# A transformer block on one core: the third part of each output block, the loads of key stacks and the key differences placed behind the maxima's parts, with SyncE's queue in the program's order during attention

## The chip, the cores and the metric

The kernel runs on one core of one Trainium2 chip. The metric is the device time of one execution in microseconds; the time before is the median of three runs. A profile is one execution recorded by the hardware profiler, and all rows below are from it. The engines are PE (TensorE), DVE (VectorE), ACT (ScalarE) and POOL (GpSimd); SP (SyncE) only issues DMAs here.

## The reference

One transformer block on 2048 rows of 576 numbers:

```
x  = A_x
h  = x + attention(layernorm(x), wqkv, wo)      # 32 heads of 18 columns, full softmax
h2 = h + (gelu(n @ w_gate) * (n @ w_up)) @ w_down    with n = layernorm(h), 4608 hidden columns
```

The result is float32. The kernel gets this accuracy with pairs of float16 numbers (high and low part), and with seven products in place of eight in the second half.

## The kernel before, in words

The program has three stages. Up to about 203 us it normalises the rows and makes queries, keys and values. Then comes attention, up to about 1405 us, and then the gated products to the end.

**Attention** is a loop over 32 blocks, n = 4g + qc: eight groups g of four heads, and in each group four blocks qc of 512 queries. A block has 16 steps kt, one for each 128 keys. In a step PE makes the scores of the four heads (`score`, L704, into PSUM banks), ACT takes their exponentials (L714, L716), and PE multiplies them with the values (`weigh`, L725) into two accumulators.

The exponentials need the largest score of each query ahead of time. `maxima` is a generator that runs one and a half blocks ahead of the scores: PE makes products (`max_bank`, L642), DVE takes their maxima (L656, L654), and ACT helps with L650. In step kt = 9 of block n the first piece taken from it calls `max_finish(n + 1)`: one more reduction on DVE (L667), three small operations that scale and split the result (L670 to L672, on POOL), a DMA that transposes it (L674, tile mT), and four small DMAs that put it into two extra rows of the query stacks (L680, A<-mT or W<-mT). The first score of block n + 1 reads these rows.

**Output of a block** is `out_block(n)`, a generator in three parts, run during block n + 1. Part one copies the accumulators (L739 on ACT, L741 on DVE), adds them on POOL (L742) and fetches the row of sums as tile rc with a DMA (L747). Part two inverts the sums (POOL, L754 to L758; in the last four blocks DVE, L760), writes them to DRAM (L762) and reads them back spread over partitions (L763, nat<-rc). Part three multiplies with them and splits the result (POOL, L767 to L769; in the last two blocks DVE, L771 to L773), and writes it to its place in X with four to nine DMAs (L782, L785, L786). Before, part two is taken behind step kt = 3 and part three behind kt = 5 (kt = 6 from block 29 on).

**Key stacks.** `load_stacks(g + 1)` issues 12 DMAs on SP and 12 on POOL (L593, L594), `load_ends` 8 on SP (L615), and `key_steps` five POOL operations (L622 to L625), 8 DMAs to DRAM (L628, kd<-nat) and 3 back (L630, nat<-kd). They fill the set of the next group; the first to read it are its maxima, from block 4g + 2, step 9 on.

**Behind the maxima.** From block 30, step 9 on, there are no maxima left, and each step takes one product of the output matrix: `wo_pairs` for 8 row tiles, then `wo_block(2)` for 4 more from step 15 of block 31 on. Both are `wo_tiles`: its local `fetch` (L849) loads a row tile of x into one of two buffers, `xbs` (one in A, one in WK). The tile's two products (L325) are added to it by DVE (L859), and then tile k + 2 is fetched. The products of `wo_pairs` use one PSUM bank in turn, those of `wo_block(2)` four. `rows` cuts finished rows into float16 parts on DVE (L917 to L921) and turns them with DMA transposes (L947).

**What sets the order.** PE, ACT, DVE and POOL run in the order in which the program is written. SP's queue does so up to L1312 and again from L1382 on, behind the loop. In between, a scheduler orders SP's DMAs by its own estimate: it may issue a DMA earlier than it is written. Each queue runs strictly in order: a DMA whose data is not ready holds up those behind it.

Of the kernel before, what the change touches and what calls it, by code (L numbers as in the profile page):

```python
# [28 lines left out]
MSC = 4096.0  # L29
# [3 lines left out]
def tile_block(  # L33
# [18 lines left out]
    nc = tc.nc  # L52
# [4 lines left out]
    NT = S // P  # L57
    TB = min(512, S)
    NB = S // TB
# [6 lines left out]
    NG = H // 4  # L66
# [16 lines left out]
    def of_pair(ins, banks, write):  # L83

        x = ins.ins
        mine = str(x.engine)
        for e in sorted(engines_of_pair - {mine}):
            keep = [o for b in banks for group in last_use[b][: 1 + write] for o in group if str(o.engine) == e]
            tc.declare_no_dep(x, group=f"pair_{e}", keep=keep, reason="the other bank of the pair")
        tc.add_to_no_dep_group(f"pair_{mine}", x)  # L90
        engines_of_pair.add(mine)
        return x
# [234 lines left out]
    def run(it):  # L327
        for _ in it:
            pass
# [8 lines left out]
    def take(it, n=1):  # L338
        for _ in range(n):
            next(it, None)  # L340
# [103 lines left out]
    in_order = ExitStack()  # L444
# [124 lines left out]
    def half(j, rows):  # L569
        return slice(64 * j, 64 * j + rows)  # L570
# [29 lines left out]
    LOWEST = -3.0e38  # L600
# [18 lines left out]
    def key_steps(g):  # L619

        for d, e in zip(dif, ends):
            nc.gpsimd.tensor_sub(d, e[:, 1::2], e[:, ::2])  # L622
        nc.gpsimd.tensor_add(dif[0], dif[0], dif[1])
        nc.gpsimd.tensor_copy(parts_d[0], dif[0])
        nc.gpsimd.tensor_sub(parts_d[1], dif[0], parts_d[0])  # L625
        for k, d in zip(kd, parts_d):
            for s in range(DQ):
                nc.sync.dma_start(k[:, :, s], d[s * DH : (s + 1) * DH])  # L628
        for i, k in enumerate((kd[0], kd[1], kd[0])):
            nc.sync.dma_start(steps[g % 2][i * DH : (i + 1) * DH],  # L630
                              k.rearrange("r h s i -> r h (s i)"))
# [32 lines left out]
    def max_finish(n, mx):  # L664
        g, qc = divmod(n, NB)
        m = small.tile([P, 4, TPB], F32, tag="m", name="m")
        nc.vector.tensor_reduce(m, mx.rearrange("p t h c -> p h t c"), axis=AX.X, op=ALU.max)  # L667
        mm = mms[n % 2]
        hst = mm[:, : 8 * TPB].rearrange("p (h s t) -> p h s t", h=4, s=2)
        nc.gpsimd.tensor_scalar_mul(m, m, 1 / MSC)  # L670
        nc.gpsimd.tensor_copy(hst[:, :, 0], m)
        nc.gpsimd.tensor_sub(hst[:, :, 1], m, hst[:, :, 0])  # L672
        mT = small.tile([P, 1, P], F16, tag="mT", name="mT")
        nc.sync.dma_start_transpose(mT, mm)  # L674
        for pr in range(2):
            Q = sets[g % 2][pr][0]
            for j in range(2):
                k = (4 * pr + 2 * j) * TPB
                row = 64 * j + R1
                nc.sync.dma_start(Q[row : row + 2, qc * TB : (qc + 1) * TB],  # L680
                                  mT[k : k + 2 * TPB, 0])

    NPE = 4
# [8 lines left out]
    def bank_at(i):  # L692

        return pair[:, i] if i < 2 else (singles[:3] + quads[1:2])[i - 2]

    def score(n, kt, heads, bank):

        g, qc = divmod(n, NB)
        mm = []
        for i, hh in enumerate(heads):  # L700
            pS = bank_at(bank + i)
            Q, K = sets[g % 2][hh // 2]
            r = half(hh % 2, R1 + 2)
            mm += [nc.tensor.matmul(pS[c : c + CT, :TB], K[r, kt * P + c : kt * P + c + CT],  # L704
                                    Q[r, qc * TB : (qc + 1) * TB], start=True, stop=True)
                   for c in range(0, P, CT)]
        of = tuple(range(bank, bank + len(heads)))
        if bank < 2:
            xs = [of_pair(m_, (of[k // 4],), True) for k, m_ in enumerate(mm)]
            for k, b in enumerate(of):  # L710
                wrote_pair((b,), xs[4 * k : 4 * k + 4])
        pe = pes[(2 * kt + heads[0] // 2) % NPE]
        if len(heads) == 2:
            act = nc.scalar.activation(pe, pair, AF.Exp, scale=ex_reg)  # L714
        else:
            act = nc.scalar.activation(pe[:, heads[0] % 2], bank_at(bank)[:, :TB], AF.Exp, scale=ex_reg)  # L716
        if bank < 2:
            read_pair(of, of_pair(act, of, False))

    def weigh(n, kt, accs, q):  # L720
        qs = slice(q * TB // 2, (q + 1) * TB // 2)
        for i, acc in enumerate(accs):
            ks = slice(64 * i, 64 * i + 64)
            for hh in range(4):
                nc.tensor.matmul(acc[CT * hh : CT * hh + CT, qs],  # L725
                                 Vg[n // NB][ks, kt * G4 + hh * VC : kt * G4 + hh * VC + CT],
                                 pes[(2 * kt + hh // 2) % NPE][ks, hh % 2, qs],
                                 start=(kt == 0 and q == 0), stop=(kt == NT - 1 and q == 1))
# [61 lines left out]
    NS = NG * NB  # L790
# [5 lines left out]
    def maxima():  # L796

        for n in range(NS):
            mx = small.tile([P, TPB, 4, NB], F32, tag="mx", name="mx")
            over, both = ("over", "both") if n else ("one", "one")  # L800
            if n:
                nc.gpsimd.memset(mx[:, :, 0, 1::2], LOWEST)
            for u in range(0, UPS, 2):
                t, k = divmod(u, NB)
                for unit in ((over, t, k + 1, 0), ("one", t, k, 1), ("one", t, k + 1, 1), ("one", t, k, 2),
                             ("one", t, k, 3), ("one", t, k + 1, 2), ("one", t, k + 1, 3), (both, t, k, 0)):
                    max_bank(n, mx, *unit, bank=bank_now[0])
                    yield
            max_finish(n, mx)
# [496 lines left out]
    qk_tiles(3, 4, 5)  # L1306
    load_stacks(0)
    load_ends(0)
    key_steps(0)
    load_w(of, wo, nc.gpsimd)  # L1310
    sums = chain(norm_wo(), raw_norms())
    sp_order.close()  # L1312
# [15 lines left out]
    halves = deque([None, None])  # L1328
    LAST_MAX = (NS - 1) * NT - 7
    rows = rows0()  # L1330
    for n in range(NS):
        g, qc = divmod(n, NB)
        late = n > NS - NB
        for kt in range(NT):
# [13 lines left out]
                else:  # L1348
                    take(side)
            halves += [(n, kt, accs, q) for q in range(2)]  # L1350
            if n and kt in ((2 if n == NS - 1 else 3, 6) if late else (3, 5)):
                take(ob)
            if n * NT + kt == LAST_MAX - 2:
                fill = wo_pairs(ring(singles[:1]))
# [10 lines left out]
            if g == 0 and qc == 0 and kt == NT - 1:  # L1365
                run(fill)
                init_set(sets[1])
            if g + 1 < NG and kt == 2 and qc == (1 if g == 0 and NB > 1 else 0):
                load_stacks(g + 1)
                load_ends(g + 1)  # L1370
            if g + 1 < NG and kt == 9 and qc == (1 if g == 0 and NB > 1 else 0):
                key_steps(g + 1)
            if n == 2 and kt == 4:
                side = prepare_wo()
            if n == NS - NB and kt == 2:
# [2 lines left out]
            if n == NS - NB and kt == 8:  # L1378
                side = chain(split_early(0, 0, lambda: load_matrix(w_up, 0, nc.gpsimd)), pause(2),
                             split_early(0, 1, lambda: load_matrix(w_gate, 1, nc.gpsimd)),  # L1380
                             pause(2), until_ready(second))
    in_order.enter_context(tc.manual_schedule(engines={EngineType.SP}))  # L1382
    run(side)
    for half_ in halves:
        weigh(*half_)
# [106 lines left out]
```

## Time and profile before

| | us |
|---|---|
| median of 3 runs | 2631.65 (2628.14 to 2634.61) |
| the profiled execution's own time | 2628.84 |
| its span, first to last instruction | 2627.1 |
| PE busy | 2548.7 (97%) |
| DVE busy | 2003.7 (76%) |
| ACT busy | 1651.6 (63%) |
| POOL busy | 858.0 (33%) |
| mean granted TensorE clock | 0.992 |

In the rows, "us" stamps run from the span's start. A row of the timeline gives start, length, engine, line, operation, tiles, and how often; in brackets the idle time of the engine before it and what ended it. SPq rows are DMA issues on SP's queue, not the transfers. A row of the windows gives the stretch and its length, then busy time and count for each engine, then the granted clock (PEclk), the DMA engines' share and GB/s.

### The profile page before, as it was taken

The page shows a single profiled execution, that of the slowest core. Times are in us where ns is not written, and L with a number is a line of the kernel's source. Part 1 is how long each engine was busy: PE and PEld are TensorE (multiplying, and loading weights), DVE is VectorE, ACT ScalarE, POOL GpSimd, SP SyncE. Part 2 cuts the span into 40 slices and gives each one's busy share as a digit, 9 for nine tenths or more (in the row PEclk, how much of TensorE's full clock was granted, in tenths as well). Part 3 has the DMA queues.
Part 4 walks back from the last instruction along what each step waited for, and adds up shares of the span by engine and source line. Part 5 has one row for each costly group of instructions (what it writes and reads, how often), then busy time and mean ns, then how long its engine had stood idle before and what let it go on. Part 6 is the DMA issues. An engine that isn't in the chain of part 4 may idle for free.

```text
span 2627.1 us, 96403 instructions
## 1 busy us (share of the span) xinstructions
PE 2548.7 (97%) x41245; PEld 1446.6 (55%) x41245; DVE 2003.7 (76%) x3888; ACT 1651.6 (63%) x2898; POOL 858.0 (33%) x1176
## 2 busy tenths in 40 slices
PE   8999899999999999999999999999999999999999
PEld 4645455555555555555555555555555555555555
DVE  8479899999999999999957765656565656565653
ACT  6229899999999999999965433333333333333332
POOL 4301532332323232433676432222222222222221
PEclk9999999999999999999999999999999999999999
DMA  8621010101101010101126410101010101011110
GB/s 225 153 78 46 18 47 21 43 19 32 36 18 44 18 47 21 44 20 30 29 59 130 91 34 30 34 30 34 30 34 30 34 30 34 30 33 31 33 56 36
DMA packets 170367, 120.96 MB, mean 46 GB/s; under 512 B 88664, under 2 KB 147564, under 8 KB 169938
## 3 DMA queue, kind: packets, MB, share of 16 engines
q1 hardware_dynamic: 161198, 98.47, 14.0%
q0 software_dynamic: 8608, 16.33, 2.4%
q8 instruction: 322, 5.28, 0.9%
q14 instruction: 107, 0.88, 0.1%
q10 hardware_dynamic: 132, 0.01, 0.0%
HBM read 80.05 MB, written 15.01 MB: 36 GB/s over the span
## 4 chain that ended last, share of the span: by engine, by line
PE 67%; DVE 8%; POOL 7%; issue 5%; SPq 5%; ACT 4%; DMA 4%; ACTq 0%; POOLq 0%; DVEq 0%
PE bank L1193 14%; PE more L1193 14%; PE bank L325 11%; PE more L325 8%; DVE mx L656 6%; PE bank L642 4%; ACT WK L716 3%; PE bank L725 3%; PE quad L725 3%; PE quad L325 2%; DVE nat L654 2%; PE pair L704 2%; POOL rp L754 2%; PE bank L704 1%; SPq L628 1%
## 5 line engine op out<-in xcount | busy, mean ns | idle before, releaser
L656 DVE TENSOR_REDUCE mx<-bank 128x1 f32<-128x512 f32 x1064 | 707.9, 683 | 61.9 <-PE bank L642 60.3
L725 PE MATMUL bank<-WK,V 64*32 64x256 f32 x8192 | 644.8, 383 | 11.0 <-ACT nat L739 10.5
L725 PE MATMUL quad<-WK,V 64*32 64x256 f32 x8192 | 644.2, 383 | 0.2 <-DVE nat L744 0.2
L716 ACT ACTIVATE WK<-bank 128x512 f32<-128x512 f32 x768 | 530.7, 691 | 49.4 <-PE bank L642 33.3
L1193 PEld LDWEIGHTS <-W 128*128 128x128 f16 x2394 | 234.0, 98 | 278.5
L325 PEld LDWEIGHTS <-WK 128*128 128x128 f16 x3456 | 338.2, 98 | 88.3
L716 ACT ACTIVATE WK<-quad 128x512 f32<-128x512 f32 x512 | 355.4, 694 | 16.2 <-PE bank L704 12.7
L656 DVE TENSOR_REDUCE mx<-pair 128x1 f32<-128x512 f32 x488 | 336.8, 690 | 2.9 <-PE pair L642 0.8
L714 ACT ACTIVATE WK<-pair 128x1024 f32<-128x1024 f32 x256 | 279.5, 1092 | 0.4 <-ACT WK L716 0.2
L725 PEld LDWEIGHTS quad<-WK,V 64*32 64x32 f32 x8192 | 239.5, 106 | 29.5 <-DVE nat L744 0.7
L725 PEld LDWEIGHTS bank<-WK,V 64*32 64x32 f32 x8192 | 220.4, 106 | 39.2 <-ACT nat L739 21.4
L325 PE MATMUL more<-W,WK 128*128 128x288 f16 x1728 | 235.2, 286 | 0.0
L325 PE MATMUL bank<-W,WK 128*128 128x288 f16 x1728 | 235.2, 286 | 0.0
L642 PEld LDWEIGHTS <-W 54*32 54x32 f16 x4096 | 139.3, 90 | 171.4 <-issue 111.4
L642 PEld LDWEIGHTS <-A 54*32 54x32 f16 x4096 | 131.7, 90 | 169.8 <-issue 112.5
L1193 PE MATMUL bank<-X,W 128*128 128x512 f16 x792 | 223.8, 379 | 0.0
L642 PE MATMUL bank<-W 54*32 54x512 f16 x2048 | 206.4, 389 | 6.0
L642 PE MATMUL bank<-A 54*32 54x512 f16 x2220 | 205.2, 387 | 6.1 <-DVE mx L656 0.4
L1061 POOL TENSOR_TENSOR A<-A 128x384 f32<-128x384 f32 x136 | 138.5, 1039 | 200.9 <-DMA A<-in_B_w_up_dram 117.1
L1193 PE MATMUL bank<-V,W 128*128 128x512 f16 x720 | 202.4, 379 | 0.0
L1207 POOL TENSOR_TENSOR WK<-tmp,WK 128x512 f16<-128x512 f32 x73 | 88.7, 1215 | 307.5 <-ACT WK L1204 307.2
L716 ACT ACTIVATE WK<-pair 128x512 f32<-128x512 f32 x256 | 178.6, 698 | 0.0
(360 smaller groups left out, 4952.8 us busy)
## 6 DMA issues: line engine op xcount, KB each, us to landing
A<-in_B_w_down_dram SPq DMA_DIRECT2D x8, 1152.0 KB
nat<-rc SPq DMA_DIRECT2D x32, 256.0 KB
A<-in_B_w_gate_dram SPq DMA_DIRECT2D x64, 128.0 KB
A<-in_B_w_up_dram SPq DMA_DIRECT2D x64, 128.0 KB
qk_hi<-tmp SPq DMA_DIRECT2D x36, 128.0 KB
qk_lo<-tmp SPq DMA_DIRECT2D x36, 128.0 KB
out_dram<-nat SPq DMA_DIRECT2D x16, 288.0 KB
X<-nat SPq DMA_DIRECT2D x100, 36.0 KB
```

What stands on the lines that cost most here:

```text
L325: nc.tensor.matmul(dst, a, b, start=(i == 0), stop=(i == len(pairs) - 1))
L642: mm = [nc.tensor.matmul(pm[c : c + CT, :TB], Q[r, q0 + c : q0 + c + CT], keys, start=True, stop=True) for c in range(0, P, CT)]
L654: nc.vector.tensor_tensor_reduce(row, pm[:, :TB], row, 1.0, LOWEST, ALU.add, ALU.max, dst)
L656: red = nc.vector.tensor_reduce(dst, pm[:, :TB], axis=AX.X, op=ALU.max)
L704: mm += [nc.tensor.matmul(pS[c : c + CT, :TB], K[r, kt * P + c : kt * P + c + CT], Q[r, qc * TB : (qc + 1) * TB], start=True, stop=True) f ...
L714: act = nc.scalar.activation(pe, pair, AF.Exp, scale=ex_reg)
L716: act = nc.scalar.activation(pe[:, heads[0] % 2], bank_at(bank)[:, :TB], AF.Exp, scale=ex_reg)
L725: nc.tensor.matmul(acc[CT * hh : CT * hh + CT, qs], Vg[n // NB][ks, kt * G4 + hh * VC : kt * G4 + hh * VC + CT], pes[(2 * kt + hh // 2) % ...
L754: nc.gpsimd.tensor_tensor(rc[:, c : c + 4], den[:, c : c + 4], minus_one.to_broadcast([P, 4]), op=ALU.pow)
L1061: op(W8[:, d], W8[:, a], W8[:, b])
L1193: nc.tensor.matmul(bank, w, x_, start=start and i == 0, stop=i == len(mm) - 1, skip_group_check=not start)
L1207: nc.gpsimd.tensor_sub(hl[:, 2 * i + j], v, hh[:, 2 * i + j])
```

## The change

Six edits, of which no one alters what is computed:

- Part three of `out_block` is taken behind step kt = 9 in place of 5 (blocks 30 and 31 keep 6). Since `max_finish` runs at the start of step 9, it now stands ahead of part three on POOL and on SP.
- `load_stacks` and `load_ends` move from step 2 of block 4g to step 10 (for the first group they stay at step 2 of block 1).
- `key_steps` moves from step 9 of block 4g to step 10 of block 4g + 1, and its three DMAs that read back follow at step 13.
- For the last two blocks the three small operations of `max_finish`, and for the last one a memset, go from POOL to DVE.
- SP's queue is held to the program's order from the start of the attention loop on, in place of from behind it.
- An assertion in Python (`weighed`) is added; it makes no instruction.

```
@@ key_steps
                 nc.sync.dma_start(k[:, :, s], d[s * DH : (s + 1) * DH])
+        yield
         for i, k in enumerate((kd[0], kd[1], kd[0])):
@@ max_finish
-        nc.gpsimd.tensor_scalar_mul(m, m, 1 / MSC)
-        nc.gpsimd.tensor_copy(hst[:, :, 0], m)
-        nc.gpsimd.tensor_sub(hst[:, :, 1], m, hst[:, :, 0])
+        by = nc.gpsimd if n < NS - 2 else nc.vector
+        by.tensor_scalar_mul(m, m, 1 / MSC)
+        by.tensor_copy(hst[:, :, 0], m)
+        by.tensor_sub(hst[:, :, 1], m, hst[:, :, 0])
@@ maxima
-                nc.gpsimd.memset(mx[:, :, 0, 1::2], LOWEST)
+                (nc.gpsimd if n < NS - 1 else nc.vector).memset(mx[:, :, 0, 1::2], LOWEST)
@@ ahead of the attention loop
-    key_steps(0)
+    run(key_steps(0))
...
+    in_order.enter_context(tc.manual_schedule(engines={EngineType.SP}))
     for n in range(NS):
@@ in the loop
-            if n and kt in ((2 if n == NS - 1 else 3, 6) if late else (3, 5)):
+            if n and kt in (2 if n == NS - 1 else 3, 6 if n > NS - 3 else 9):
                 take(ob)
...
-            if g + 1 < NG and kt == 2 and qc == (1 if g == 0 and NB > 1 else 0):
+            if g + 1 < NG and (qc, kt) == ((1, 2) if g == 0 else (0, 10)):
                 load_stacks(g + 1)
                 load_ends(g + 1)
-            if g + 1 < NG and kt == 9 and qc == (1 if g == 0 and NB > 1 else 0):
-                key_steps(g + 1)
+            if g + 1 < NG and qc == 1 and kt == 10:
+                steps_made = key_steps(g + 1)
+                take(steps_made)
+            if g + 1 < NG and qc == 1 and kt == 13:
+                run(steps_made)
@@ behind the loop
-    in_order.enter_context(tc.manual_schedule(engines={EngineType.SP}))
     run(side)
```

The order of PE and ACT does not change at all. Lines behind 629 have higher numbers in the changed kernel: L674 is now L676, L680 L682, L747 L755, L767 L775, L782 L790, L785 L793, L849 L857, L947 L955.

The first place is SP's queue over one ordinary block, before:

```order
L747 DMA rc<-nat 128x1x16
L762 DMA rc_862<-rp 128x16
L763 DMA nat<-rc_862 128x1x512
L782 DMA X<-nat 18x2x512 x3
L782 DMA X<-nat 2x2x512
L782 DMA X<-nat 16x2x512
L674 DMA_TRANSPOSE mT<-mm_858 128x1x128
L680 DMA W<-mT 2x4x128 x4
```

and now:

```order
L755 DMA rc<-nat 128x1x16
L770 DMA rc_862<-rp 128x16
L771 DMA nat<-rc_862 128x1x512
L676 DMA_TRANSPOSE mT<-mm_858 128x1x128
L682 DMA W<-mT 2x4x128 x4
L790 DMA X<-nat 18x2x512 x3
L790 DMA X<-nat 2x2x512
L790 DMA X<-nat 16x2x512
```

The transpose of the maxima and the four DMAs of its parts now stand ahead of the DMAs to X.

The second place is POOL in the same kind of block, before:

```order
L754 TENSOR_TENSOR rp<-rc,minus_one 128x4 x4
L756 TENSOR_TENSOR re<-rc,rp 128x16
L757 TENSOR_SCALAR re<-re 128x16
L758 TENSOR_TENSOR rp<-rp,re 128x16
L767 TENSOR_TENSOR nat<-nat 128x512
L768 CAST nat<-nat 128x512
L769 TENSOR_TENSOR nat<-nat 128x512
L670 TENSOR_SCALAR m<-m 128x16
L671 CAST mm_858<-m 128x4x4
L672 TENSOR_TENSOR mm_858<-m,mm_858 128x4x4
```

and now:

```order
L762 TENSOR_TENSOR rp<-rc,minus_one 128x4 x4
L764 TENSOR_TENSOR re<-rc,rp 128x16
L765 TENSOR_SCALAR re<-re 128x16
L766 TENSOR_TENSOR rp<-rp,re 128x16
L672 TENSOR_SCALAR m<-m 128x16
L673 CAST mm_858<-m 128x4x4
L674 TENSOR_TENSOR mm_858<-m,mm_858 128x4x4
L810 MEMSET mx 128x4x2
L775 TENSOR_TENSOR nat<-nat 128x512
L776 CAST nat<-nat 128x512
L777 TENSOR_TENSOR nat<-nat 128x512
```

The three small operations on the maxima have moved ahead of part three's.

The third place is SP's queue in blocks 30 and 31, where x is fetched for the output products. Before, the first two fetches are issued long ahead, one among the DMAs of the first stage and one in block 27; in block 30 there stand only the next ones:

```order
L785 DMA X<-nat 18x512
L786 DMA X<-nat 18x512
L674 DMA_TRANSPOSE mT<-mm_858 128x1x128
L680 DMA W<-mT 2x4x128 x4
L849 DMA A<-in_A_x_dram 128x576
L849 DMA WK<-in_A_x_dram 128x576
```

and now the first two stand behind block 30's nine DMAs to X:

```order
L793 DMA X<-nat 18x512
L794 DMA X<-nat 18x512
L857 DMA A<-in_A_x_dram 128x576
L857 DMA WK<-in_A_x_dram 128x576
L676 DMA_TRANSPOSE mT<-mm_858 128x1x128
L682 DMA W<-mT 2x4x128 x4
```

Likewise the first two fetches of `wo_block(2)`, at the end of block 31. Now they come behind the transposes of the last row tile's first part:

```order
L955 DMA_TRANSPOSE V<-V 128x15x128
L955 DMA_TRANSPOSE X<-tmp_82 128x9x128 x2
L955 DMA_TRANSPOSE V<-tmp_82 128x2x128
L857 DMA A<-in_A_x_dram 128x576
L857 DMA WK<-in_A_x_dram 128x576
```

Before, one of them stood right behind the DMAs to X and one ahead of the second row tile's second part:

```order
L785 DMA X<-nat 18x512 x3
L849 DMA A<-in_A_x_dram 128x576
L947 DMA_TRANSPOSE V<-tmp_82 128x2x128
L947 DMA_TRANSPOSE X<-tmp_82 128x9x128 x2
L849 DMA WK<-in_A_x_dram 128x576
L947 DMA_TRANSPOSE V<-V 128x15x128
```

Both have moved down the queue, behind the rows of all four tiles' first parts.

More of the change, by code (lines that the diff above doesn't have):

```diff
@@ L694, in bank_at @@
         return pair[:, i] if i < 2 else (singles[:3] + quads[1:2])[i - 2]
+    weighed = set()
     def score(n, kt, heads, bank):
         g, qc = divmod(n, NB)
+        k2 = n * NT + kt - NPE // 2
+        assert k2 < 0 or {(k2, 0), (k2, 1)} <= weighed
         mm = []
@@ L720, in weigh @@
     def weigh(n, kt, accs, q):
+        weighed.add((n * NT + kt, q))
         qs = slice(q * TB // 2, (q + 1) * TB // 2)
```

## The prediction

> **What bounds the kernel now.** I read the page first, then PE's waits, then the windows and timelines of attention.
>
> ```profile
> span 2627.1 us, 96403 instructions
> PE 2548.7 (97%) x41245; PEld 1446.6 (55%) x41245; DVE 2003.7 (76%) x3888; ACT 1651.6 (63%) x2898; POOL 858.0 (33%) x1176
> ```
>
> PE is idle for 78 us of the span at most. The change touches attention and the stretch behind it, so I ask who makes PE wait there. The view of PE's waits gives for each pair the total, the times and the longest:
>
> ```profile
> PE bank L704 <- DMA A<-mT: 17.0, 7, 6.3
> PE bank L704 <- DMA W<-mT: 16.7, 7, 4.0
> ```
>
> At 14 of the 31 block changes the first score waits for the maxima's parts, 33.7 us in all. What a wait costs in the end is read from whole blocks. A block has 16 x 16 = 256 score products on L704, so the count tells how many blocks lie in a stretch:
>
> ```profile
> 239.30:1305.45 1066.15, 621.02 (x7424) 233.98 (x7423) 0.99 0.12 31
> 1160.00:1230.50 70.50, 43.07 (x512) 16.15 (x512) 1.00 0.08 22
> 722.80:758.90 36.10, 21.78 (x256) 8.34 (x260) 0.93 0.07 17
> ```
>
> Blocks 1 to 29 take 1066.15 us; blocks 26 and 27, without a wait at either end, 35.25 each. 29 x 35.25 = 1022.25, so the waits cost **43.9 us** over these blocks, more than their 33.7: after a wait the pipeline refills and the clock is low (third row: block 14 has no wait within, starts with a clock of 0.93 and takes 0.85 us more than a clean block).
>
> Why a part is late, at the start of block 14 (timelines of DVE, POOL, SP, PE):
>
> ```profile
> 703.01 0.22 DVE L667 TENSOR_REDUCE m<-mx 128x16 f32<-128x64 f32 x1
> 709.93 1.28 POOL L767 TENSOR_TENSOR nat<-nat 128x512 f32<-128x512 f32 x1 [8.05 <-DMA nat<-rc]
> 713.21 0.26 POOL L670 TENSOR_SCALAR m<-m 128x16 f32<-128x16 f32 x1
> 713.82 0.23 POOL L672 TENSOR_TENSOR mm<-m,mm 128x16 f16<-128x16 f32 x1
> 713.15 4.12 SPq L782 DMA_DIRECT2D X<-nat  x5
> 717.38 1.14 SPq L674 DMA_TRANSPOSE mT<-mm  x1
> 719.67 2.75 SPq L680 DMA_DIRECT2D W<-mT  x4
> 722.83 0.61 PE L704 MATMUL bank<-W 56*32 56x512 f16 x4 [4.00 <-DMA W<-mT]
> ```
>
> DVE has the maxima at 703.23. POOL comes to them 10 us later, since part three (L767) stands ahead and waits for nat<-rc. Then the transpose stands behind five DMAs to X for another 3.3 us.
>
> **The change part by part.**
>
> *Part three behind the maxima; SP in order.* From the maxima the path is now POOL 0.84 (713.21 to 714.05), transpose to first small DMA 2.29 (717.38 to 719.67), the four issues 2.75, landing 0.41 (722.42 to 722.83): 6.3 us, so ready at 709.6. The block would start at 722.83 - 4.00 = 718.8: 9 us to spare. The tightest block is 3, where POOL also works on the output matrix:
>
> ```profile
> 296.65 0.22 DVE L667 TENSOR_REDUCE m<-mx 128x16 f32<-128x64 f32 x1
> 312.01 0.25 POOL L670 TENSOR_SCALAR m<-m 128x16 f32<-128x16 f32 x1
> 318.29 0.61 PE L704 MATMUL bank<-A 56*32 56x512 f16 x2 [6.32 <-DMA A<-mT]
> ```
>
> Ready there at 296.9 + 6.3 = 303.2 if POOL were free, against a start at 312.0. POOL first has pieces of the output matrix, some 7 us of the spare 9; I count it as just in time. Part three itself, 4 steps later, feeds X, which is read only from block 30 on. So I take the whole 43.9 us, and 0.8 for block 30, which also starts after a wait: **-44.7**. The bounds are 33.7 (refill stays) and 44.7. DVE and ACT cap it already: the clean blocks are clean with them.
>
> *Maxima's last parts on DVE.* Seven small operations; on POOL they take 0.2 to 0.26 us each, so under 2 us of DVE at two places, of which block 30's lie where DVE waits for PE. **+0.5**, bounds 0 and 2.
>
> *Stacks and key differences.* In a block 4g, SP now issues 20 more DMAs behind those to X:
>
> ```profile
> 792.77 0.30 SPq L593 DMA_DIRECT2D W<-qk_hi  x1
> 802.68 0.84 SPq L615 DMA_DIRECT2D nat<-qk_hi  x1
> ```
>
> 12 x 0.32 + 8 x 0.8 = 10.2 us. With the transpose, parts and X (2.3 + 2.8 + 4.1) they end 20 us after DVE's maxima, which come 15 us ahead of the next block: 5 us into it, about when part one's L747 is due (728.82 in block 14, 6 us in). Their cover is the 9 us above; without it each late us is a us of PE. First reader of the stacks is a block and a half later. **0**, bounds 0 and 5.
>
> *SP in order at block 30: a new wait.* The scheduler had issued the first two loads of x far ahead. Now they stand behind block 30's DMAs to X:
>
> ```profile
> 1195.24 0.36 SPq L849 DMA_DIRECT2D A<-in_A_x_dram  x1
> 1326.32 1.17 POOL L769 TENSOR_TENSOR nat<-nat 128x512 f16<-128x512 f32 x1
> 1326.27 0.83 SPq L785 DMA_DIRECT2D X<-nat  x1
> 1332.59 0.70 SPq L786 DMA_DIRECT2D X<-nat  x1
> 1331.05 0.52 DVE L859 SCALAR_TENSOR_TENSOR nat<-bank,u_o,A 128x288 f32<-128x288 f32 x1 [3.51 <-PE bank L325]
> 1332.43 0.30 PE L325 MATMUL bank<-W,X 128*128 128x288 f16 x1
> 1344.40 0.36 SPq L849 DMA_DIRECT2D A<-in_A_x_dram  x1
> 1347.27 0.52 DVE L859 SCALAR_TENSOR_TENSOR nat<-bank,u_o,A 128x288 f32<-128x288 f32 x1 [3.92 <-DMA A<-in_A_x_dram]
> ```
>
> In the old times: the first DMA to X now carries both halves and waits for L769 (1327.5); nine take 7.0 us (1326.27 to 1333.29), so x is asked for at 1334.5 and, as at 1344.40, used 2.9 us later: L859 at 1337.4 in place of 1331.05. The one PSUM bank is free at 1337.9; PE wanted it at 1332.43. **Wait of 5.5 us.** Nothing hides it:
>
> ```profile
> 1329.00:1402.00 73.00, 70.35 (x1286) 39.63 (x1280) 38.59 (x90) 44.68 (x80) 50.60 (x92) 1.00 0.39 86
> 540.20:543.60 3.40, 3.40 (x72) 1.95 (x70) 2.08 (x4) 2.56 (x4) 0.00 (x0) 0.50 0.06 14
> 540.09 0.56 PE L704 MATMUL bank<-A 56*32 56x512 f16 x3 [1.77 <-DMA A<-mT]
> ```
>
> From 1329 on PE has work all the time (70.35 of 73) while DVE and ACT idle. And a wait of 1.77 us is followed by 3.4 us at a clock of 0.50. On a full PE that is 1.7 us more; for the longer wait I take 2.0. The stall at 1347.27 goes (PE lost 0.3 by it). **+7.2**, bounds 0 (x in time) and 10.
>
> *The same behind block 31: a second one.*
>
> ```profile
> 1386.03 0.41 SPq L849 DMA_DIRECT2D A<-in_A_x_dram  x1
> 1402.37 1.88 PE L325 MATMUL bank<-W,X 128*128 128x288 f16 x14
> 1404.36 0.51 DVE L859 SCALAR_TENSOR_TENSOR nat<-bank,u_o,A 128x288 f32<-128x288 f32 x1
> 1406.92 5.31 PE L325 MATMUL bank<-W,X 128*128 128x288 f16 x42
> 1407.10 2.77 SPq L947 DMA_TRANSPOSE X<-tmp  x2
> 1408.50 0.46 DVE L917 CAST V<-V 128x576 f16<-128x576 f32 x1 [3.63 <-DMA V<-V]
> 1410.42 0.51 DVE L859 SCALAR_TENSOR_TENSOR nat<-quad,u_o,A 128x288 f32<-128x288 f32 x1
> 1412.63 0.94 DVE L859 SCALAR_TENSOR_TENSOR nat<-bank,u_o,WK 128x288 f32<-128x288 f32 x2
> 1417.21 1.67 PE L1193 MATMUL more<-X,A 128*128 128x512 f16 x7
> ```
>
> The load issued at 1386.03 now stands behind the transposes of 1407.10, so at 1409.9; with 2.9 us to its use, as at 1344.40, L859 comes at 1412.8, not 1404.36. With four banks PE does four products, and wants the first bank back for the fifth at 1406.92 + 2 x 1.72 = 1410.4 (three took 5.31, each starts 1.72 behind the last); it gets it at 1413.3, **2.9 us** late. Then DVE's own queue paces the rest, with 1.9 us of work ahead of the second L859 (1408.50 to 1410.42) and 2.2 ahead of the third (to 1412.63): products six to eight start at 1415.7, 1417.9 and 1419.6, and the gated products at 1421.3 in place of 1417.2: 4.1 us. With 1.2 for the low clock, partly covered by DVE, **+5.3**, bounds 0 and 10.
>
> [...]
>
> **Sum.** -44.7 + 0.5 + 0 + 7.2 + 5.3 = -31.7 us. Behind it PE is busy throughout, so all of it reaches the end. The profiled execution took 2628.84, the median is 2631.65: 2597.1 and **2600**.
>
> **Rivals.**
>
> *The new waits are hidden (chance 0.18).* If both loads land in time, as they would if SP ran ahead of PE there, the two terms go: 2631.65 - 44.2 = 2587. For it: DMAs are lightly used in block 30 (0.39). Against: the nine DMAs to X need L769, which nothing moves up.
>
> *The new waits are larger (0.13).* Both at their upper bound, and the first loses the low clock twice: +10 +10 +4 against -44: 2612. For it: the second falls where transposes fill the queue. Against: a load is one DMA of 0.4 us.
>
> *No change (0.05).* The parts come just as late, because POOL or SP is held by something else in its queue. Block 3 could; the others have 9 us. Then 2631, plus at most the 12 of the new waits if all failed.
>
> *Slower (0.04).* SP's queue in blocks 4g and 4g + 1 runs over: if the 20 DMAs there wait for one another, L747, then part two on POOL, then the maxima behind it come late. It decides once L747 is over 9 us late; each us beyond costs 14 us over 14 blocks, so past 9 + 31.7 / 14 = 11.3 us the gain is gone, and at 13 us late it is 2600 + 56 = 2656. Against: issues took 0.30 to 0.84 us each.
>
> **How the numbers follow.** The forecast has 0.60, its own range 2591 to 2608. Two measurements of this kernel tell about 0.3% (8 us) apart. Faster 0.91, within 0.05, slower 0.04. The range runs from the first rival to the second: 2585 to 2613.
>
> **What would show it.** Right: no wait of PE on mT; blocks 1 to 29 at 35.3 us, 1023 in all; a wait of L325 of about 5 us in block 30 with L859 waiting for A<-in_A_x, another of about 3 some 75 us later; the stretch from 1417 on as long as before. Wrong: mT still among PE's waits (POOL or SP held), blocks over 35.5 without one (another bound), or no wait on L325, which leaves 2587.

## The result, and the profile after

The changed kernel takes **2604.56 us** (median of 4 runs, 2602.72 to 2606.57) against 2630.95 before (4 runs, 2628.14 to 2634.61): a ratio of 0.9899, 95% interval 0.9882 to 0.9916. That is 26.4 us less; forecast were 31.7, with a range of 2585 to 2613. The profiled execution of the changed kernel took 2606.57 us, the highest of its four, the one before 2628.84, under its median; the two profiles differ by 22.5 us of span, and the stages below add up to that.

The view of PE's waits (engine, tile and line, what it waited for: us in total, times, longest):

```profile
PE bank L325 <- DVE nat L867: 9.7, 2, 5.9
PE bank L710 <- DVE mx L657: 2.5, 3, 1.8
PE bank L643 <- DVE mx L657: 1.5, 3, 1.1
```

No wait on mT is left (33.7 us before). The two waits of L325 on x are there, and DVE now holds PE up on L657. The windows give the stages, cut at the first score of blocks 1, 30 and 31 and at the first gated product, first of the changed kernel, then of the one before (PE alone: stretch, length, busy time and count, clock, DMA share, GB/s):

```profile
239.40:1270.12 1030.72, 1001.16 (x29709) 1.00 0.13 33
1270.12:1324.59 54.47, 47.21 (x1015) 0.94 0.20 53
1324.59:1393.16 68.57, 63.01 (x1040) 0.98 0.47 100
1393.16:2604.50 1211.34, 1204.75 (x7146) 1.00 0.14 39
```
```profile
239.37:1305.51 1066.14, 1009.96 (x29709) 0.99 0.12 31
1305.51:1353.83 48.32, 47.23 (x1002) 0.94 0.17 46
1353.83:1417.21 63.38, 61.58 (x1039) 1.00 0.57 115
1417.21:2627.05 1209.84, 1204.44 (x7146) 1.00 0.14 38
```

| stage | forecast | measured |
|---|---|---|
| blocks 1 to 29 | -43.9, and about +0.5 for DVE | -35.4 |
| block 30 | -0.8 + 7.2 = +6.4 | +6.15 |
| block 31 to the first gated product | +5.3 | +5.2 |
| from there to the end | 0 | +1.5 |

The parts of the maxima ahead of block 14, changed kernel, on DVE, POOL, SP and PE:

```profile
685.87 0.22 DVE L668 TENSOR_REDUCE m<-mx 128x16 f32<-128x64 f32 x1
686.19 0.25 POOL L672 TENSOR_SCALAR m<-m 128x16 f32<-128x16 f32 x1 [4.36 <-DVE m L668]
687.04 1.14 SPq L676 DMA_TRANSPOSE mT<-mm  x1
689.33 2.74 SPq L682 DMA_DIRECT2D W<-mT  x4
692.18 4.16 SPq L790 DMA_DIRECT2D X<-nat  x5
701.30 0.39 PE L710 MATMUL bank<-W 56*32 56x512 f16 x4
```

POOL follows DVE at once, where it came 10 us later before; the last part is issued by 692.07, 6.0 us behind the maxima (6.3 were worked out) and 9.2 us ahead of the block, which starts at 701.30.

In block 29 something else ends last. DVE, POOL and PE there:

```profile
1252.09 0.82 DVE L672 TENSOR_SCALAR m<-m 128x16 f32<-128x16 f32 x1
1252.94 0.18 DVE L673 CAST mm<-m 128x16 f16<-128x16 f32 x1
1253.15 0.68 DVE L674 TENSOR_TENSOR mm<-m,mm 128x16 f16<-128x16 f32 x1
1250.68 2.20 POOL L1131 TENSOR_SCALAR A<-A,p_s_m 128x768 f32<-128x768 f32 x1
1252.95 0.85 POOL L1132 CAST A<-A 128x768 f16<-128x768 f32 x1
1254.49 0.62 PE L710 MATMUL bank<-W 56*32 56x512 f16 x4 [1.78 <-DVE mx L657]
```
```profile
1254.53:1257.95 3.42, 3.42 (x68) 0.50 0.07 15
```

The operations on sixteen numbers per partition take DVE 0.82 and 0.68 us. L672 ends at 1252.91, just behind POOL's L1131 (1252.88); L674 ends at 1253.83, just behind POOL's L1132 (1253.80). PE then waits 1.78 us for DVE's next maximum, and the 3.4 us behind it run at half clock: block 29 takes 39.25 us, 4.0 over a clean one.

The two new waits, on SP, DVE and PE (changed kernel):

```profile
1296.83 0.70 SPq L794 DMA_DIRECT2D X<-nat  x1
1297.76 0.34 SPq L857 DMA_DIRECT2D A<-in_A_x_dram  x1
1301.09 0.52 DVE L867 SCALAR_TENSOR_TENSOR nat<-bank,u_o,A 128x288 f32<-128x288 f32 x1 [9.54 <-DMA A<-in_A_x_dram]
1301.66 3.52 PE L325 MATMUL bank<-W,X 128*128 128x288 f16 x14 [5.90 <-DVE nat L867]
...
1379.91 1.25 SPq L955 DMA_TRANSPOSE V<-tmp  x1
1381.21 0.57 SPq L857 DMA_DIRECT2D A<-in_A_x_dram  x1
1384.46 0.52 DVE L867 SCALAR_TENSOR_TENSOR nat<-bank,u_o,A 128x288 f32<-128x288 f32 x1 [9.26 <-DMA A<-in_A_x_dram]
1385.03 3.15 PE L325 MATMUL bank<-W,X 128*128 128x288 f16 x14 [3.76 <-DVE nat L867]
1395.21 0.94 DVE L867 SCALAR_TENSOR_TENSOR nat<-bank,u_o,WK 128x288 f32<-128x288 f32 x2 [2.51 <-DMA WK<-in_A_x_dram]
```

Each load of x is issued right behind the DMAs that the forecast named, and used 3.3 us later; the last row is a later load, late by 2.51 us. From the traces alone the theory is: the place of part three gives the gain; SP's order makes two waits on x; DVE's small operations, held up by POOL, spoil block 29. The experiments undo or add one of these at a time.

### The profile page after: what moved, and what is told of

Same layout as the page of the kernel before. It is cut to its first block, busy times and chain, and to the rows that moved or that the text cites. A ratio compares the mean times of both kernels' runs of the same rounds, so it can differ in the third digit from the quotient of the medians.

```text
span 2604.5 us, 96416 instructions
## 1 busy us (share of the span) xinstructions
PE 2542.3 (98%) x41245; PEld 1445.7 (56%) x41245; DVE 2006.7 (77%) x3895; ACT 1648.6 (63%) x2898; POOL 856.0 (33%) x1169
## 4 chain that ended last, share of the span: by engine, by line
PE 73%; DVE 14%; ACT 7%; issue 3%; DMA 2%; POOL 1%; SPq 0%; ACTq 0%; DVEq 0%; POOLq 0%
PE bank L1201 14%; PE more L1201 14%; PE bank L325 11%; DVE mx L657 10%; PE more L325 8%; PE bank L643 6%; ACT WK L722 5%; PE bank L733 4%; PE quad L733 4%; DVE nat L655 3%; PE quad L325 3%; PE pair L710 2%; PE bank L710 2%; PE pair L325 1%; PE quad L643 1%
## 5 line engine op out<-in xcount | busy, mean ns | idle before, releaser
L657 DVE TENSOR_REDUCE mx<-bank 128x1 f32<-128x512 f32 x1064 | 707.1, 682 | 26.5 <-PE bank L643 24.3
L722 ACT ACTIVATE WK<-bank 128x512 f32<-128x512 f32 x768 | 537.1, 699 | 16.6 <-PE pair L710 13.7
L325 PEld LDWEIGHTS <-WK 128*128 128x128 f16 x3456 | 338.2, 98 | 88.3
L657 DVE TENSOR_REDUCE mx<-pair 128x1 f32<-128x512 f32 x488 | 336.3, 689 | 3.4 <-PE pair L643 1.3
L643 PEld LDWEIGHTS <-W 54*32 54x32 f16 x4096 | 140.7, 89 | 181.4 <-issue 119.8
L325 PE MATMUL more<-W,WK 128*128 128x288 f16 x1728 | 235.2, 286 | 0.0
L325 PE MATMUL bank<-W,WK 128*128 128x288 f16 x1728 | 235.2, 286 | 0.0
L643 PEld LDWEIGHTS <-A 54*32 54x32 f16 x4096 | 132.7, 89 | 176.3 <-issue 117.8
L643 PE MATMUL bank<-W 54*32 54x512 f16 x2048 | 203.8, 384 | 8.2 <-DVE mx L657 1.1
L643 PE MATMUL bank<-A 54*32 54x512 f16 x2220 | 203.5, 384 | 6.7 <-DVE mx L657 0.4
```

The lines of the kernel that those rows point to most:

```text
L325: nc.tensor.matmul(dst, a, b, start=(i == 0), stop=(i == len(pairs) - 1))
L643: mm = [nc.tensor.matmul(pm[c : c + CT, :TB], Q[r, q0 + c : q0 + c + CT], keys, start=True, stop=True) for c in range(0, P, CT)]
L657: red = nc.vector.tensor_reduce(dst, pm[:, :TB], axis=AX.X, op=ALU.max)
```

## The experiments

Every run is beside runs of the kernel before on the same chip (its median 2628.7 to 2629.3 there; 2630.95 beside the changed kernel, so that a difference of about 2 us between a run's median and the changed kernel's shows nothing). Stages are cut as above, from the profiled execution of each run; the changed kernel is 1030.7, 54.5, 68.6 and 1211.3. A profiled execution lay within 3.3 us of its run's median, but in "before, SP in order" it was the longest of four, 11.1 us over it.

| | median | ratio (95%) | blocks 1-29 | 29 alone | block 30 | 31 to gated | rest |
|---|---|---|---|---|---|---|---|
| x early in block 30 | 2596.74 | 0.9871 (0.9855-0.9888) | 1031.9 | 38.9 | 46.6 | 68.0 | 1211.6 |
| x early in block 31 | 2597.99 | 0.9876 (0.9860-0.9893) | 1030.4 | 39.0 | 54.9 | 63.4 | 1210.0 |
| small operations on POOL | 2602.96 | 0.9896 (0.9880-0.9913) | 1031.4 | 38.2 | 54.1 | 67.9 | 1210.5 |
| block 29 cleared, on POOL | 2603.93 | 0.9904 (0.9887-0.9920) | 1026.9 | 35.9 | 56.3 | 69.3 | 1211.0 |
| POOL quiet, on DVE | 2604.17 | 0.9904 (0.9887-0.9920) | 1028.9 | 36.7 | 54.0 | 70.4 | 1209.8 |
| part three at step 5 | 2647.93 | 1.0067 (1.0048-1.0086) | 1078.6 | 40.7 | 53.9 | 67.9 | 1208.9 |
| before, SP in order | 2671.27 | 1.0155 (1.0136-1.0175) | 1107.5 | 41.9 | 55.8 | 68.7 | 1208.9 |
| changed, SP scheduled | 2598.35 | 0.9882 (0.9865-0.9899) | 1036.9 | 45.3 | 47.6 | 63.4 | 1209.1 |
| before, part three alone | 2592.80 | 0.9861 (0.9844-0.9877) | 1029.0 | 38.0 | 47.8 | 63.4 | 1208.4 |
| stacks at the old place | 2607.03 | 0.9915 (0.9898-0.9931) | 1032.6 | 37.1 | 55.1 | 68.5 | 1209.3 |
| x early twice, 29 cleared | 2590.11 | 0.9851 (0.9834-0.9867) | 1028.0 | 36.0 | 46.6 | 63.6 | 1210.7 |
| part three alone, 29 cleared | 2589.41 | 0.9847 (0.9833-0.9860) | 1028.4 | 35.9 | 46.6 | 63.6 | 1208.9 |

### The two loads of x

```
             if n * NT + kt == LAST_MAX - 2:      # changed
             if n * NT + kt == LAST_MAX - 7:      # x early in block 30
```

> The changed kernel with one edit: the first two loads of x for the output products are issued at step 2 of block 30, ahead of that block's DMAs to X, in place of step 7, behind them. Theory (the 5.9 us wait of L325 in block 30 is set by where these loads stand on SP's queue): no wait of L325 in block 30, the low clock there goes with it, block 30 takes 47.5 to 48.5 us instead of 54.47, and the median is 6 to 7 us under that of the changed kernel (2604.6): 2598. Rival (PE is held there anyway, by DVE or by the one PSUM bank, so a load in time moves the stall and no more): block 30 stays within 1.5 us of 54.5 or block 31 gets longer by as much, median 2604 +- 2.

The wait in block 30 is gone, 7.8 us by the medians (6 to 7 were expected). What is left on L325 is the wait behind block 31; block 30, from its own stamps:

```profile
PE bank L325 <- DVE nat L867: 3.7, 2, 3.4
```
```profile
1270.17:1316.77 46.60, 45.22 (x1015) 1.00 0.22 62
```

```
+            if n == NS - 1 and kt == 9:
+                next_fill = wo_block(2, m_ring)
+                take(next_fill)
...
-                fill = wo_block(2, m_ring)
-                take(fill)
+                fill = next_fill
```

> The changed kernel with one edit: the last four row tiles' generator is made, and its first two loads of x issued, at step 9 of block 31 in place of step 14, ahead of the transposes. Theory (the 3.76 us wait of L325 behind block 31 is set by these loads' place on SP's queue): that wait goes with its 3.4 us of half clock; from the start of block 31 to the first gated product it takes 63.4 us, as before, instead of 68.6; the 0.95 us wait of the first gated product on the same tiles goes too; median 2598 to 2599. Rival (the transposes or DVE's own queue set the end of that stretch): 68 us stay, median 2604 +- 2.

```profile
1324.82:1388.19 63.37, 61.58 (x1039) 1.00 0.52 111
```

This stretch is back at its 63.4 us, and the rest at 1210.0. That the 1.5 us lost behind the first gated product belong to this wait as well is not shown: four of the runs below keep a second wait of 2.7 to 4.7 us and spend only 1208.9 to 1209.8 us on the rest. Both loads' places on SP's queue set these waits; PE was not held otherwise.

### What costs block 29 its 4 us

```
-        by = nc.gpsimd if n < NS - 2 else nc.vector
+        by = nc.gpsimd
...
-                (nc.gpsimd if n < NS - 1 else nc.vector).memset(mx[:, :, 0, 1::2], LOWEST)
+                nc.gpsimd.memset(mx[:, :, 0, 1::2], LOWEST)
```

> The changed kernel with one edit undone: the three small operations on the maxima of the last two blocks, and the memset of the last, run on POOL again. Theory (on DVE these operations cost block 29 its 4 us, because they take 0.82, 0.18 and 0.68 us there beside a POOL operation and DVE is what PE waits for): the 1.78 us wait of PE on DVE L657 in block 29 goes, and block 29's own steps run at the pace of the others; but POOL comes to the operations only behind its two matrix pieces of that block, so that the parts of block 30 are 1 to 2 us late: block 29 takes 36.5 to 38, and the median is 2602 to 2604. Rival 1 (these operations are not the cause, DVE is late there for another reason): the wait on L657 stays and the wait on mT is added: block 29 takes 40.5 or more, median 2606 or more. Rival 2 (POOL is in time too): block 29 at 35.4, median 2600.5.

```profile
1262.24 0.25 POOL L672 TENSOR_SCALAR m<-m 128x16 f32<-128x16 f32 x1
1270.22 0.40 PE L710 MATMUL bank<-W 56*32 56x512 f16 x4 [1.87 <-DMA W<-mT]
```

DVE's delay is gone, and a wait of 1.87 us on mT stands in its place: POOL reaches the maxima (there at 1253.25) only at 1262.24, behind its matrix pieces. Block 29 takes 38.2 us, a little over the 36.5 to 38 expected. So the choice of engine for these operations is worth about 1 us of block 29 (39.25 against 38.16); what costs is POOL's load in this block, and either engine pays for it. The next run takes that load away:

```
-                else:
+                elif n != NS - 3 or kt not in (6, 7, 8):
                     take(side)
```

with the small operations of block 30's maxima on POOL again.

> The changed kernel with block 29 cleared: the matrix pieces that POOL and DVE would work on in steps 6 to 8 of block 29 are left for later steps, and the small operations on the maxima of block 30 and the memset are on POOL (those of block 31 stay on DVE). Theory (what costs block 29 its 4 us is DVE's delay by the small operations beside a busy POOL, and POOL with nothing ahead of them does them in time): no wait of PE on L657 nor on mT in block 29, no half clock at 1254 us, block 29 takes 35.3 to 35.6, median 2600 to 2601. Rival (the pieces put off run into block 30 or the stretch behind it and cost there what was saved): block 29 at 35.4, but later stretches longer by 2 us or more, median 2604 +- 1.5.

```profile
1228.92:1264.86 35.94, 35.11 (x1037) 1.00 0.15 37
1264.86:1321.14 56.28, 47.53 (x1015) 0.91 0.20 51
1321.14:1390.41 69.27, 63.08 (x1039) 0.98 0.46 99
```

Block 29 comes close to the theory, 35.9 us (35.3 to 35.6 were expected); the median is as the rival says. Of the 3.3 us saved, 2.5 are given back in the two stretches behind it: PE reaches the output products earlier, the loads of x don't come as much earlier, and the waits of L325 grow to 7.3 and 4.3 us. It is not the pieces put off, which the rival named, that take the time back, but the waits on x: with the loads early as well (three edits together, below), block 30 takes 46.6 us with the same pieces put off.

The last of these runs leaves the small operations on DVE and only keeps POOL's matrix pieces away (`kt not in (4, 5, 6, 7, 8)`, nothing else).

> The changed kernel with the matrix pieces of steps 4 to 8 of block 29 put off, so that POOL computes nothing while DVE has the small operations on the maxima of block 30, which stay on DVE. Theory (L672 and L674 took 0.82 and 0.68 us on DVE because each waited for the end of a POOL operation): they take 0.17 to 0.36 us each, the wait of PE on DVE L657 in block 29 falls from 1.79 to under 0.7 us, no half clock follows, and block 29 takes 35.5 to 36.3 us instead of 39.25; the waits on x in blocks 30 and 31 grow as when the block was cleared before, so that the median is 2602 to 2605. Rival (these operations are slow on DVE by themselves): L672 keeps 0.8 us or DVE stays late for another reason, and block 29 stays at 38.5 or more.

```profile
1252.34 0.35 DVE L672 TENSOR_SCALAR m<-m 128x16 f32<-128x16 f32 x1
1252.93 0.17 DVE L674 TENSOR_TENSOR mm<-m,mm 128x16 f16<-128x16 f32 x1
1251.49 1.16 POOL L777 TENSOR_TENSOR nat<-nat 128x512 f16<-128x512 f32 x1
```

The same operations take 0.17 us once POOL has stopped, and the one that met POOL (L672, beside L777 until 1252.65) again ends just behind it. DVE comes to L672 equally far into block 29 in both kernels (21.22 us) and is through with L674 0.97 us earlier here; PE's wait is shorter by the same 0.97 us, 0.81 in place of 1.78 (under 0.7 was expected). No half clock follows, and block 29 takes 36.7 us, a little over the 36.3 expected. So POOL's work makes DVE late, and DVE makes PE late.

In the changed kernel L672 and L674 each end 0.03 us behind the end of an operation of POOL (1252.91 and 1252.88, 1253.83 and 1253.80); L673 shows no such wait there (0.18 us, begun 0.01 us ahead of POOL's L1132). Nor is the operation that meets POOL always the one that takes long: in the run with the stacks at the old place L672 takes 0.17 us (from 1256.00) beside POOL's L1131 (1254.62 to 1256.85), and L673 is the one that ends behind it (0.67 us, to 1256.88). Which of the small operations is held, and why, stays open; that POOL holds DVE up does not, by the 0.97 us of the run above.

### Which edit carries the gain

Part three put back behind step 5, all else as changed:

```
-            if n and kt in (2 if n == NS - 1 else 3, 6 if n > NS - 3 else 9):
+            if n and kt in (2 if n == NS - 1 else 3, 6 if n > NS - NB else 5):
```

> The changed kernel with its first edit alone undone: part three is taken behind step 5 again (6 in the last three blocks, as before), so that POOL's multiplication and the DMAs to X stand ahead of the maxima's parts; SP stays in the program's order, stacks, key differences and the last blocks stay as changed. Theory (the gain of 35 us in blocks 1 to 29 is the place of part three ahead of or behind the parts, on POOL and SP): PE waits on mT again at a dozen block changes or more, blocks 1 to 29 take 1060 to 1070 us instead of 1030.7, and with the new waits on x kept the median is 2635 to 2645. Rival (the gain comes from the order of SP or from the stacks and key differences): no or few waits on mT, median 2605 to 2612.

```profile
PE bank L710 <- DMA A<-mT: 23.0, 8, 5.9
PE bank L710 <- DMA W<-mT: 18.2, 8, 3.8
```

Sixteen waits on mT return, 41 us: the place of part three it is. The time, 2647.9, is 3 us over the range given, and these blocks are slower than those of the kernel before by 12.5 us; what the program's order on SP does to them is seen in the next run, the kernel before with SP in order:

```
+    in_order.enter_context(tc.manual_schedule(engines={EngineType.SP}))
     for n in range(NS):
```

> The kernel before with one edit alone: SP is held to the program's order during attention. Theory (the order by itself brings nothing, since part three is written ahead of the parts, and it costs the late loads of x): PE waits on mT at as many block changes as before (14, 34 us), blocks 1 to 29 take 1060 to 1072 us, waits of L325 on x appear in block 30 and behind block 31 unless the late start of block 30 covers them, and the median is 2632 to 2643. Rival (the scheduler's order of SP was what made the parts late): most waits on mT go, median 2600 to 2612.

```profile
239.71:1347.23 1107.52, 1018.81 (x29709) 0.96 0.13 31
```
```profile
371.91 4.48 SPq L615 DMA_DIRECT2D nat<-qk_hi  x4
376.96 3.09 SPq L615 DMA_DIRECT2D nat<-qk_lo  x4
380.15 0.41 SPq L762 DMA_DIRECT2D rc<-rp  x1
387.31 1.28 POOL L767 TENSOR_TENSOR nat<-nat 128x512 f32<-128x512 f32 x1 [12.16 <-DMA nat<-rc]
```

Both theories missed: 2671.3, 28 us over the upper end. In the profiled execution the program's order alone costs 41.4 us in blocks 1 to 29. That execution was 11.1 us over the median; by the medians the run is 42.4 us slower than the kernel before with the two waits on x included, which leaves some 30 us to these blocks (an estimate: 42.4 less the 11.8 by which the other stages differ). In each block 4g the twenty loads for the next group are written ahead of part two's DMAs; in block 4 they end at 380.1, so L762 is issued at 380.15. In the kernel before, L762 of the same block is issued at 371.39, since the scheduler had put off most of the L615 behind it:

```profile
371.39 0.36 SPq L762 DMA_DIRECT2D rc<-rp  x1
```

Block 4 itself starts 1.55 us later here (355.93 against 354.38), so L762 comes 7.2 us later into the block. With part three ahead of the maxima, these 7.2 us go through POOL to the parts, and at the six blocks 4g + 1 from block 5 on PE waits 6.9 to 8.2 us (7.73 at block 5). The move of stacks and key differences takes this away (with the small edits to the last blocks): 29 us of blocks 1 to 29 by the profiles, 23 us by the medians (2671.3 to 2647.9), as long as part three stands ahead.

The other way round, the changed kernel with SP left to the scheduler during attention:

> The changed kernel with one edit undone: SP's queue is ordered by the scheduler during attention, as before, all other edits kept. By the built order the transposes of the maxima still stand ahead of nearly all DMAs to X up to block 28, and the loads of x are issued far ahead again. Theory (the gain is part three's place; the program's order on SP brings only the two waits on x): no waits on mT in blocks 1 to 28, blocks 1 to 29 at 1029 to 1034 us, no wait of L325 over 1 us, median 2590 to 2596. Rival (SP's order is needed for the gain: single DMAs to X ahead of the transposes hold them up): waits on mT return in several blocks, median 2604 or more.

```profile
PE bank L710 <- DMA W<-mT: 7.2, 1, 7.2
```

No mT wait up to block 29 and none on x, as expected, but one of 7.2 us at the start of block 30, where the scheduler's queue has DMAs to X ahead of the transpose; that is why the median is 2 us over the range. The program's order removes this one (block 29 39.25 in place of 45.3) and makes the two on x (6.9 and 5.2 us); it costs 6.2 us on balance by the medians (4.5 by the ratios, whose intervals overlap). Then the first edit alone, on the kernel before:

```
-            if n and kt in ((2 if n == NS - 1 else 3, 6) if late else (3, 5)):
+            if n and kt in (2 if n == NS - 1 else 3, 6 if n > NS - 3 else 9):
```

> The kernel before with the first edit alone: part three behind step 9 (6 in the last two blocks); SP ordered by the scheduler, stacks, key differences and the last blocks' small operations as before. Theory (this edit alone carries the gain; the others add nothing to it under the scheduler's order): PE waits on mT only at the start of block 30 (5 to 7 us: POOL reaches the maxima's small operations behind its matrix pieces, and DMAs to X stand ahead of the transpose there), blocks 1 to 29 take 1034 to 1039 us, no wait of L325 on x over 1 us, median 2595 to 2601, that is under the changed kernel's 2604.6. Rival (the stacks and key differences have to be moved too, or the small operations to DVE): waits on mT in blocks 4g and 4g + 1, blocks 1 to 29 over 1045 us, median 2606 or more.

```profile
239.51:1268.51 1029.00, 999.78 (x29709) 1.00 0.12 32
```
```profile
1268.51 0.40 PE L704 MATMUL bank<-W 56*32 56x512 f16 x4 [1.73 <-DMA W<-mT]
```

It carries all of the gain, and more: 2592.8, 12 us under the changed kernel (10 by the ratios) and 2 under what was expected, since the one wait on mT left is 1.7 us and not 5 to 7. One thing came otherwise than expected: L325 waits 1.55 us at 1310.31, for the load of the third row tile of x, issued at 1306.21. The stacks and key differences, put back in the changed kernel:

> The changed kernel with the stacks and key differences issued where they were before (step 2 and step 9 of block 4g), all else as changed, SP in the program's order. Theory (with part three behind the parts these 31 DMAs are covered wherever they stand: by the rows of the kernel before with SP in order, L615 ends 24 us into block 4g and part two's DMAs follow 3 us later, so that the parts would be through about 3 us ahead of the block's end): no wait on mT, blocks 1 to 29 within 3 us of 1030.7, median 2602 to 2608. Rival (under the program's order they must be moved, as the comparison of the two runs with part three at step 5 suggests, 1107.5 us against 1078.7): waits on mT in some of the blocks 4g + 1, 2 us or more each, median 2612 or more.

No wait on mT is left (blocks 1 to 29 take 1032.6 us). With part three behind the parts their place is worth 2.5 us by the medians, in intervals that overlap.

### Two versions that beat both kernels

The changed kernel with both early loads and block 29 cleared:

> The changed kernel with three edits together: the first loads of x early in block 30, those of the last four row tiles early in block 31, and block 29 cleared as in the run before. Alone they gave 2596.7, 2598.0 and 2603.9, against 2604.6. Theory (the 3.3 us saved in block 29 alone were taken back by the two waits on x, which got longer by 1.4 and 0.5 us with PE earlier; with the loads in time they stay saved): block 29 at 35.9, block 30 at 46.6, from block 31 to the first gated product 63.4, the rest 1210; median 2604.6 - 7.8 - 6.6 - 3.3 = 2587. Rival (another wait in blocks 30 and 31, such as DVE's queue, takes up what comes early): one of these three stretches stays as long as in the changed kernel, median 2591 to 2596.

2590.1, 3 us over the theory and under the rival. All three stretches are as short as they were one at a time. By the medians the two early loads alone account for it (2604.6 - 7.8 - 6.6 = 2590.2); that the cleared block adds to them is seen in its stage (36.0 us), not in the medians. And the first edit alone with the cleared block:

> The kernel before with the first edit alone (part three behind step 9) and block 29 cleared: the matrix pieces of its steps 6 to 8 are left for later steps. Theory (under the scheduler's order the loads of x come in time whatever block 29 does, so that the time saved there stays saved): POOL has the maxima's parts by 1253, no wait on mT at the start of block 30, block 29 at 35.9 us instead of 38.0, the rest as with the first edit alone, median 2592.8 - 2.1 = 2590.7. Rival (the pieces put off, or the transposes behind POOL's part three in block 30, come late and give it back): block 30 or the stretch behind it longer by 1.5 us or more, median 2592 to 2595.

2589.4, 0.9847 of the time before: block 29 at 35.9, no wait on mT, none on x. It is the lowest median of all, but its interval overlaps with that of the first edit alone (2592.8) and with that of the three edits (2590.1); both versions lie clear of the changed kernel.

## Why the prediction was right, and where it was not

The time fell into the range, 4.6 us over the forecast, and the direction and the three large terms are of the mechanism forecast. That it came so close is in part luck: by the two profiles the stages add up to -22.5 us, 9.2 short of the -31.7 forecast, while the medians lie 26.4 apart, since the changed kernel's profile was its slowest execution (2.0 over its median) and the other one was 2.1 under its median.

- **Part three behind the maxima: the mechanism right, the size too large.** No wait on mT is left, and undoing this edit brings them back, doing it alone gives all of the gain. Of the 43.9 us for blocks 1 to 29 came 35.4. The 8.5 us missing lie in block 29 (4.0), block 3 (36.46 us, 1.2 over), block 1 (36.22, 1.0 over) and the other 26, which average 35.34 and not 35.25 (2.3). The step that failed is "I take the whole 43.9": it carried two of the cleanest blocks over to all 29. The 35.4 lie within the term's own bounds (33.7 to 44.7). The forecast also named a sign of being wrong, blocks over 35.5 us without a wait on mT, and seven show it: 1, 3, 5 (35.53), 7 (35.51), 13 (35.73), 21 (35.70) and 29. In blocks 3 and 29 DVE is what bounds PE; for the others the cause stays open.
- **Maxima's last parts on DVE (+0.5, bounds 0 and 2): the term that was mis-sized.** The durations were taken from POOL's rows, 0.2 to 0.26 us. Beside a POOL that works they are 0.82 and 0.68, and DVE is what PE waits for in block 29, where the step looked for cover in block 30 only. Block 29 lost 4.0 us; on POOL it would have lost 2.9, so the edit itself is about 1 us to the bad, and the rest is POOL's load, which no term had.
- **Block 3 "just in time":** yes. The last of its parts is issued 1.8 us ahead of its first score, and there is no wait on mT; the 1.2 us that this block is over are a wait of L643 on DVE, 1.09 us.
- **Stacks and key differences (0): right, with this reason.** With the old place the blocks have no wait on mT. What the step did not see is that this move is the price of SP's order: without part three's move it is worth 23 us by the medians, 29 by the profiles.
- **SP in order, two new waits (+7.2 and +5.3): right in place and size.** Waits of 5.90 and 3.76 us where 5.5 and 2.9 were worked out, and +6.15 and +5.2 us by stage where +6.4 and +5.3 were; the waits were 0.4 and 0.9 us longer than worked out, so that the stages agree better than the steps behind them. Loads issued earlier take both away. Not seen: about 1.5 us behind the first gated product, where L867 waits 2.51 us more for a load into WK and PE 0.95 us for L867; with the loads of block 31 early the rest is 1210.0, but four other runs with the second wait lose nothing there, so that the cause stays open.
- **The rivals.** That the new waits are hidden did not come true; without them the kernel would take 2590.2 by the two runs that removed one each, where 2587 was worked out. That SP's queue runs over in blocks 4g did not happen to the changed kernel; the kernel before with SP in order shows that this rival's place was well chosen: there L762 comes 7 us later into block 4, and some 30 us are lost by the medians (41 in the profiled execution).

## What to carry to other kernels

Put what a neighbour engine waits for ahead of what nobody waits for, on each queue that both pass: here that one move was worth 36 us, and the other edits together gave 10 to 12 of them back. When a scheduler's order is replaced by the program's, go through what it had hoisted; each such DMA (x here, part two's behind the stack loads there) needs a written place of its own. And price an operation that changes engine by rows of the new engine beside the neighbour that runs at that moment, not by its rows on the old one: here 0.82 and 0.68 us on DVE, where POOL's rows gave 0.2 to 0.26.

## What was unexpected of the hardware

DVE's operations on 16 numbers per partition took 0.17 to 0.18 us where POOL did not hold them up, and up to 1.09 us beside it (L673 at 1286.27, block 29 cleared, on POOL). Sixteen of them took over 0.6 us in these runs; fifteen of these ended within 0.04 us of the end of an operation of POOL (the other one is L673 at 1288.97 of "POOL quiet").

Whether a short wait of PE is followed by half clock is not a matter of its length alone. With part three at step 5, a wait of 1.66 us was followed by 3.4 us at a clock of 0.50, and one of 1.85 us by 3.4 us at 1.00:

```profile
727.33 0.40 PE L710 MATMUL bank<-W 56*32 56x512 f16 x4 [1.66 <-DMA W<-mT]
728.54:731.95 3.41, 3.41 (x72) 0.50 0.05 10
1060.31 0.40 PE L710 MATMUL bank<-W 56*32 56x512 f16 x4 [1.85 <-DMA W<-mT]
1060.30:1063.70 3.40, 2.92 (x84) 1.00 0.00 1
```

Five kernels keep the small operations on DVE beside a busy POOL in block 29, and have the same wait there, 1.78 or 1.79 us; four went to half clock behind it (0.50 from 1254.53 to 1257.95 in the changed kernel), the fifth (SP scheduled) did not (1.00 from 1254.60 to 1258.00). (A sixth, with the stacks at the old place, has a wait of 1.14 us, and none followed.)

In the traces of the two kernels and the twelve runs the cases part better by the idle time within steps of the clock than by the length of a wait. In each of them the changes of the granted clock lie whole multiples of 3.4133 us apart, to within 5 ns. Cut into such steps, from 210 us to 15 us before the end, 9680 steps ran at full clock. All 46 of them in which PE was idle for 1.90 us or more were followed by a step at half clock, and none of those with 1.55 us or less was; of the ten in between (1.66 to 1.89 us) eight were. In the two kernels alone these are 1384 steps: eleven with 1.77 to 3.41 us idle, each followed by 0.50, and 1373 with 1.54 us or less, none of them followed by it. A wait that lies across the end of a step is shared out between two: the one of 3.38 us that is left with x early in block 30 falls into two steps with 1.89 and 1.54 us idle, and no half clock followed. What parts the ten cases in between is not shown; no run was made that moves a wait against these steps and changes nothing else.

The forecast took 1.2 us for a low clock behind its second wait, from the row at 540.09. That wait came out at 3.76 us, to 1385.03, and the clock was 0.50 from 1384.24 to 1387.65; in other runs the same wait was 2.72, 2.94 and 3.24 us long (part three at step 5, small operations on POOL, stacks at the old place), and half clock followed each time.
